# The planner's latency between dependent operations of one engine set to zero, and six products of constants instead of eight

## The chip, the cores and the metric

The kernel runs on one core of one Trainium2 chip. The metric is the device time of one execution in microseconds; a comparison uses the median of several executions. The profiler's record of one more execution, the profiled one, gives the rows that are read below.

## The reference

Three layers stand one behind the other; all inputs and outputs are 32-bit or wider floats.

```python
def phi(x):                                   # q, k: (4, 8, 576, 64)
    proj = np.einsum('bhsd,df->bhsf', x, w_phi)
    proj = proj - np.max(np.abs(proj), axis=-1, keepdims=True)
    return np.concatenate([np.exp(proj), np.exp(-proj)], axis=-1)
q_p, k_p = (phi(q), phi(k))
kv = np.einsum('bhsf,bhsd->bhfd', k_p, v);  z = np.sum(k_p, axis=2)
attn = einsum('bhsf,bhfd->bhsd', q_p, kv) / (einsum('bhsf,bhf->bhs', q_p, z)[..., None] + 1e-06)
# second: a mixture of 8 experts, each token to the expert of its largest logit
h = np.maximum(x[mask] @ w1[e], 0.0);  out[mask] = gate_w * eom * (h @ w2[e])
# third: RMS norm and a gated feed-forward layer, 512 -> 1536 -> 512
g = xn @ w_gate;  y = (g * sigmoid(g) * (xn @ w_val)) @ w_out
```

The second layer's x is the first layer's output, 2304 rows of 512.

## The kernel before, in words

The program is written as a graph of tasks, which a planner in Python (class `Graph`) puts into an order when the kernel is built. The hardware has no part in that: each engine gets a fixed list of instructions, and semaphores hold an instruction until what it reads has been written.

A task has an engine, an estimated duration, the buffers that it reads and writes, and a priority. `emit` (lines 122 to 148) repeats one step: for each engine it looks at the tasks whose inputs are planned, takes the one with the smallest (possible start, priority, number), and of the five engines' candidates emits the one that can start first. A task is ready at the end of its producer plus `lat(producer's engine, own engine)`. `LAT` has 0.27 us for PE, 0.14 for ACT and DVE, 0.15 for POOL and 0 for SP; another 0.12 is added where the consumer is PE. The latency is 0 where both are on PE.

Phase 1 covers the first two layers, batch by batch (four batches), in one graph, so that the planner mixes the attention of batch b+1 with the expert products of batch b. The steps of one batch's attention that the text speaks of:

- L418 is a projection: 8 matmuls of a pair of heads with w_phi into a PSUM tile `pq` of two banks. There are two of these at first (pq0 and pq1), and one after the ninth use. L422 (DVE) takes the maximum over 128 columns, L424 (DVE) subtracts it and writes `d`. L424 is what frees `pq` for the next projection.
- For keys, L518 and L511 (ACT) write exp to `e` and `el`, L465, L468 and L472 (DVE) add up `es`, L498 (PE) makes the kv product, L487 adds the sums, L530 (ACT) and L537 (PE) transpose, L540 (DVE) copies to `kv`.
- For queries, L210 (PE) transposes `d`, L439 (ACT) takes exp into `qp`, L585 (PE; L552 for the rest of 64 rows) multiplies with `kv`, and L447, L449 and L451 (DVE: add, reciprocal, multiply) divide into `x`. L210 or L561 (PE) transposes `x`, L596 or L565 (ACT) casts it and L598 or L568 (DVE) writes the remainder of that cast; both go into `xh`.
- `guess` (L611 to L629) finds the expert that most of the 64 leftover rows choose: a PE product, L615 and L617 on DVE, the PE product L619, and L621, L623, L626, L627 and L629 on DVE. L627 writes the number that L759 loads to address the expert weights.
- `gate` (L644 to L717) takes the logits; its first products need the whole `xh`.
- The expert products are L733 and L742 (PE), 12 matmuls of 288 columns a group; L763 (ACT) and L764 (DVE) split the weights, L780 (ACT) and L782 (DVE) the hidden rows.

At the very start `warm` (L334) gives PE eight products of a matrix of constants, before the first projection. That projection reads w_phi, which L299 loads in two halves, one for each half of the partitions.

Phase 2 is the third layer, in a graph of its own (L921 and L939 on PE). Between the phases all engines load a flag and branch on it (L974 and L975); with these inputs the branch is not taken.

Of the kernel before, what the change touches and what calls it, by code (L numbers as in the profile page):

```python
# [41 lines left out]
class Graph:  # L42
# [31 lines left out]
                del self.leaving[b.tag]  # L74

    def lat(self, a, b):
        if a == b == "PE":
            return 0.0
        return self.LAT[a] + (0.12 if b == "PE" else 0.0)

# [957 lines left out]
def build(tc, ctx, q, k, l, v, w_phi, wg, wo, w1, w2, mg, mv, mo, rg, out):  # L1038
    kk = K(tc, q, k, l, v, w_phi, wg, wo, w1, w2, mg, mv, mo, rg, out)
    nc, g = tc.nc, kk.g  # L1040
    kk.consts(ctx)
    kk.psum()
    moe = ExitStack()
    att = ExitStack()
    kk.moe_slots(moe, ctx)
    kk.attn_slots(att)
    last = []
    with tc.manual_schedule():
        kk.warm(8)
        for b in range(B):  # L1050
            n = len(g.tasks)
            xh, xp, os = kk.attn(b, b * 100)
            last += g.tasks[n:]
            g.marks = getattr(g, "marks", []) + [(n, len(g.tasks))]
            cB = kk.gate(b, xh, xp, os, b * 100 + 30)
            kk.moe(b, xh, xp, cB, 1000 + 100 * b)
        n = B * E
        g.t("DVE", 0.09, lambda: nc.vector.tensor_reduce(
            out=kk.flagf[0:1, n:n + 1], in_=kk.flagf[0:1, 0:n].unsqueeze(1), axis=AX.X, op=ALU.add),
            rw=[kk.flagB], prio=400)  # L1060
        g.t("DVE", 0.07, lambda: nc.vector.tensor_copy(kk.flags[0:1, 0:n + 1], kk.flagf[0:1, 0:n + 1]),
            r=[kk.flagB], prio=400)
        g.emit(until=last)
        att.close()
        kk.phase2_slots(ctx)
        g.slot("xn", kk.xn)
        g.slot("pgv", [kk.last[:, 0]])
        for f in range(NPRE):
            kk.decode_gv(g, f, 2000 + f)
        kk.kept = g.buf("xh", hold=True)  # L1070
        kk.wgv += [Buf(None, 0) for _ in range(NKEEP)]
        for f in range(NPRE, NPRE + NKEEP):
            kk.decode_gv(g, f, 2000 + f, [kk.kept])
        yB, kk.yB = kk.yB, kk.yB[0:1]
        xn0 = kk.prep(g, 0, 355, hold=True)
        kk.yB = yB
        g.emit()
    kk.yB = []
    kk.general([x.ap for x in xn0])
    moe.close()  # L1080
    banks = kk.psum2(ctx)
    p = kk.pool(ctx, "p2", side="right")
    g = Graph()
    kk.use_phase2(g)
    kk.wgv = [Buf(None, x.ap) for x in kk.wgv[:NPRE]] + [
        Buf(None, kk.part(f)) for f in range(NPRE, NPRE + NKEEP)] + [
        Buf(None, p.tile([P, 2, 2, NC, P], F32R, name=f"wgv{f}")) for f in range(NPRE + NKEEP, NF)]
    kk.wout = [Buf(None, p.tile([P, 2, DM], F32R, name=f"wo{f}")) for f in range(NF)]
    g.slot("a", [p.tile([P, 2, UT], F32R, name=f"a{i}") for i in range(NA)])
    g.slot("po", banks[0:4])  # L1090
    g.slot("pgv", banks[4:8])
    held = [x.ap for x in xn0]
    g.slot("xn", [a for a in kk.xn if not any(a is h for h in held)])
    xn = []
    for i, a in enumerate(held):
        x = Buf("xn", a)
        x.slot = (0.0, 100 + i, a)
        xn.append(x)
    with tc.manual_schedule():
        order = [0, NU - 1] + list(range(1, NU - 1))  # L1100
        for u in range(NU):
            if u == 0:
                for f in range(NF):
                    kk.decode_o(g, f, 20 + 2 * f - 6)
                    if f >= NPRE + NKEEP:
                        kk.decode_gv(g, f, 20 + 2 * f - 13)
            kk.unit(g, u, order[u], xn, u * 100 + 20)
            if u + 1 < NU:
                xn = kk.prep(g, order[u + 1], u * 100 + 32)
        g.emit()  # L1110
# [31 lines left out]
```

## Time and profile before

| | |
|---|---|
| median of 3 executions | 857.47 us (856.54 to 859.73) |
| the profiled execution's own time | 854.88 us |
| its span, first to last instruction | 853.3 us |
| PE busy | 839.5 us, 98% of the span |
| DVE busy | 461.1 us, 54% |
| ACT busy | 306.1 us, 36% |
| phase 1 on PE | from the start to 394 us |

PE's records overlap, so its busy time says only that PE had a matmul under way. DVE's and ACT's busy times are those of their instructions. What PE waited for is in a view of its own.

### The profile page before, as it was taken

What the parts mean: (1) busy time and instruction counts of PE and PEld (TensorE: products, weight loads), DVE (VectorE), ACT (ScalarE), POOL (GpSimd) and SP (SyncE); (2) the same over time, 40 slices, a digit from 0 to 9 for tenths busy, and PEclk for the clock granted to TensorE, in tenths of its full rate; (3) what the DMA queues carried; (4) which work ended last, traced back from release to release, by engine and by line L of the source; (5) the groups of instructions that cost most, each with busy time, mean ns of one, the idle gap of its engine ahead of it and who ended that gap; (6) DMA issues with size and microseconds to landing.
All of it is one profiled execution on the core that took longest, in us unless ns stands there. A gap on an engine that the chain in (4) does not pass through costs nothing.

```text
span 853.3 us, 15129 instructions
## 1 busy us (share of the span) xinstructions
PE 839.5 (98%) x6434; PEld 725.5 (85%) x6435; DVE 461.1 (54%) x838; ACT 306.1 (36%) x523; POOL 3.0 (0%) x20
## 2 busy tenths in 40 slices
PE   7989999999999999999999999999999999999998
PEld 6878898898899999998888899888788888888886
DVE  6787786787975598972858734321414114311111
ACT  4363453344443374642435433321214122211111
POOL 1000000000000000000000000000000000000000
PEclk9999999999999999999999999999999999999999
DMA  7263325324102848743324320200002000010001
GB/s 214 82 211 124 84 74 205 118 85 174 52 27 82 310 124 251 224 128 113 116 75 149 99 99 1 61 14 0 1 1 98 1 1 1 0 50 1 0 1 50
DMA packets 64042, 74.64 MB, mean 87 GB/s; under 512 B 9312, under 2 KB 50912, under 8 KB 63456
## 3 DMA queue, kind: packets, MB, share of 16 engines
q1 hardware_dynamic: 63664, 73.27, 26.6%
q8 instruction: 53, 0.87, 0.4%
q10 hardware_dynamic: 304, 0.33, 0.1%
q14 instruction: 21, 0.17, 0.1%
HBM read 54.63 MB, written 18.96 MB: 86 GB/s over the span
## 4 chain that ended last, share of the span: by engine, by line
PE 53%; DVE 0%; ACT 0%; issue 0%
PE pz L921 35%; PE pz L939 17%; PE pz L892 0%; DVE yu L951 0%; ACT yu L954 0%
## 5 line engine op out<-in xcount | busy, mean ns | idle before, releaser
L921 PE MATMUL pz<-xn,wgv 128*128 128x512 f32 (+1 forms) x1200 | 258.2, 371 | 2.0 <-PEq L975 2.0
L921 PEld LDWEIGHTS pz<-xn,wgv 128*128 128x128 f32 x1200 | 210.1, 188 | 43.8 <-issue 2.2
L939 PE MATMUL pz<-wo,a 128*128 128x512 f32 x648 | 159.6, 394 | 0.0
L929 DVE TENSOR_TENSOR row<-pz,row 128x512 f32<-128x512 f32 (+1 forms) x60 | 38.2, 637 | 203.8 <-PE pz L921 200.2
L939 PEld LDWEIGHTS pz<-wo,a 128*128 128x128 f32 x648 | 120.9, 188 | 28.2 <-issue 1.4
L927 ACT ACTIVATE row<-pz 128x512 f32<-128x512 f32 (+1 forms) x60 | 33.4, 556 | 154.5 <-PE pz L921 154.2
L931 ACT CAST a<-row 128x512 fp32r<-128x512 f32 (+1 forms) x60 | 34.6, 577 | 120.8 <-DVE row L929 120.8
L733 PE MATMUL ph<-xh,w 128*128 128x288 f32 x528 | 77.2, 298 | 0.7 <-DVE h L782 0.7
L733 PEld LDWEIGHTS ph<-xh,w 128*128 128x128 f32 x528 | 71.5, 188 | 3.8 <-issue 2.0
L742 PE MATMUL ph<-h,w 128*128 128x288 f32 x480 | 67.9, 296 | 0.0
L742 PEld LDWEIGHTS ph<-h,w 128*128 128x128 f32 x480 | 64.5, 188 | 0.7 <-issue 0.4
L921 PE MATMUL pz<-xn,xh 128*128 128x512 f32 (+1 forms) x240 | 52.3, 373 | 0.0
L932 DVE TENSOR_TENSOR a<-row,a 128x512 fp32r<-128x512 f32 (+1 forms) x60 | 38.2, 637 | 25.8 <-ACT a L931 25.6
L422 DVE TENSOR_REDUCE m<-pq 128x8 f32<-128x1024 f32 x36 | 43.7, 1218 | 15.3 <-PE pq L418 15.1
L763 ACT CAST w<-wr 128x1024 fp32r<-128x1024 f32 x32 | 33.5, 1048 | 46.6 <-issue 19.5
L921 PEld LDWEIGHTS pz<-xn,xh 128*128 128x128 f32 x240 | 42.1, 188 | 8.9
L418 PE MATMUL pq<-wraw,qk 64*128 64x128 f32 x576 | 41.7, 286 | 4.2 <-DVE d L424 4.2
L439 ACT ACTIVATE qp<-ps 128x512 f32<-128x512 f32 x64 | 34.3, 602 | 31.4 <-PE ps L210 27.2
L764 DVE TENSOR_TENSOR w<-wr,w 128x1024 fp32r<-128x1024 f32 x32 | 39.1, 1223 | 10.0 <-ACT w L763 9.4
L424 DVE TENSOR_TENSOR d<-pq,m 128x1024 f32<-128x1024 f32 x36 | 43.6, 1216 | 0.4
L418 PEld LDWEIGHTS pq<-wraw,qk 64*128 64x128 f32 x576 | 35.3, 189 | 9.4 <-DVE d L424 5.1
L742 PE MATMUL ps<-h,w 128*128 128x288 f32 x288 | 41.6, 297 | 0.0
(151 smaller groups left out, 874.4 us busy)
## 6 DMA issues: line engine op xcount, KB each, us to landing
wr<-in_moe_w SPq DMA_DIRECT2D x32, 512.0 KB, 4.1
xdr<-xh SPq DMA_DIRECT2D x4, 2304.0 KB, 9.0
raw<-in_moe_w_gate SPq DMA_DIRECT2D x12, 512.0 KB, 4.3
raw<-in_moe_w_val SPq DMA_DIRECT2D x12, 512.0 KB, 4.0
raw<-in_moe_w_out SPq DMA_DIRECT2D x12, 512.0 KB, 3.5
qk<-in_k SPq DMA_DIRECT2D x16, 256.0 KB, 3.0
v<-in_v SPq DMA_DIRECT2D x16, 256.0 KB, 2.9
qk<-in_q SPq DMA_DIRECT2D x16, 256.0 KB, 3.0
```

The costliest lines, as they stand in the source:

```text
L418: nc.tensor.matmul(pp.ap[:, hf, k * FE:(k + 1) * FE], lhsT=t.ap[r, k], rhs=self.wraw[r], start=True, stop=True)
L422: g.t("DVE", dve(1024), lambda: nc.vector.tensor_reduce(out=m.ap, in_=pv(), axis=AX.X, op=ALU.max, apply_absolute_value=True), r=[pp], w=[ ...
L424: g.t("DVE", dve(1024), lambda: nc.vector.tensor_tensor(out=d.ap.rearrange("p h k f -> p (h k) f"), in0=pv(), in1=m.ap.unsqueeze(2).to_bro ...
L439: g.t("ACT", act(512), lambda f=f: nc.scalar.activation(qp.ap[:, f].rearrange("p c t -> p (c t)"), pd.ap, AF.Exp, scale=1.0 - 2.0 * f), r= ...
L733: self.nc.tensor.matmul(ph[:, 0:HS], lhsT=wv[:, a, c, fs], rhs=xh[:, x, c, cs], start=(c == 0 and i == 0), stop=(c == NC - 1 and i == 2))
L742: self.nc.tensor.matmul(ph[:, 0:HS], lhsT=wv[:, a, f], rhs=hs[f][:, x, cs], start=(f == 0 and i == 0), stop=(f == 7 and i == 2))
L764: g.t("DVE", dve(1024), lambda: nc.vector.tensor_tensor(out=w.ap[:, 1], in0=wr.ap, in1=w.ap[:, 0], op=ALU.subtract), r=[wr], rw=[w], prio= ...
L921: nc.tensor.matmul(ps.ap[:, 0:UT], lhsT=w[:, i, a, c], rhs=xn[c].ap[:, x, 0:UT], start=(c == 0 and n == 0), stop=(c == NC - 1 and n == 2))
L929: g.t("DVE", dve(UT), lambda sil=sil, ps=pgv[1]: nc.vector.tensor_tensor(out=sil.ap[:, 0:UT], in0=ps.ap[:, 0:UT], in1=sil.ap[:, 0:UT], op= ...
L931: g.t("ACT", act(UT, False), lambda sil=sil, a=a: nc.scalar.copy(a.ap[:, 0, 0:UT], sil.ap[:, 0:UT]), r=[sil], w=[a], prio=pr)
L932: g.t("DVE", dve(UT), lambda sil=sil, a=a: nc.vector.tensor_tensor(out=a.ap[:, 1, 0:UT], in0=sil.ap[:, 0:UT], in1=a.ap[:, 0, 0:UT], op=ALU ...
L939: nc.tensor.matmul(po[t].ap, lhsT=a.ap[:, x, ts], rhs=w[:, y], start=(f == 0 and n == 0), stop=(f == NF - 1 and n == 2))
```

## The change: what the planner assumes, and six products in `warm`

```diff
     def lat(self, a, b):
-        if a == b == "PE":
+        if a == b != "SP":
             return 0.0
         return self.LAT[a] + (0.12 if b == "PE" else 0.0)
...
     with tc.manual_schedule():
-        kk.warm(8)
+        kk.warm(6)
```

The first edit sets the planner's latency to 0 for a task that follows its producer on DVE, on ACT or on POOL. No instruction is added or removed by it; the planner's order of both phases changes with it. The second removes two instructions.

Three places of the order follow. In the names, `_0`, `_1`, ... tell the buffer: pq0 and pq1 are the two projection tiles, ps0 to ps3 single PSUM banks, m_0 to m_2 and d_0 to d_2 the maxima and differences, qk_0 to qk_5 the loaded pairs of heads.

DVE, from its first instruction on (start of batch 0), before:

```order
L422 TENSOR_REDUCE m_0_164<-pq0_85 128x8
L422 TENSOR_REDUCE m_1_165<-pq1_89 128x8
L424 TENSOR_TENSOR d_0_161<-pq0_85,m_0_164 128x1024
L424 TENSOR_TENSOR d_1_162<-pq1_89,m_1_165 128x1024
L422 TENSOR_REDUCE m_2_166<-pq0_85 128x8
L465 TENSOR_TENSOR es_0_178<-e_0_167 128x1024
L424 TENSOR_TENSOR d_2_163<-pq0_85,m_2_166 128x1024
```

and now:

```order
L422 TENSOR_REDUCE m_0_164<-pq0_85 128x8
L424 TENSOR_TENSOR d_0_161<-pq0_85,m_0_164 128x1024
L422 TENSOR_REDUCE m_1_165<-pq1_89 128x8
L424 TENSOR_TENSOR d_1_162<-pq1_89,m_1_165 128x1024
L465 TENSOR_TENSOR es_0_178<-e_0_167 128x1024
L422 TENSOR_REDUCE m_2_166<-pq0_85 128x8
L424 TENSOR_TENSOR d_2_163<-pq0_85,m_2_166 128x1024
```

Each subtraction now stands directly behind its own maximum, and the sum es_0 ahead of the third maximum.

DVE in batch 0, from the projections of the queries on (behind the division that writes the second half of the first x), before:

```order
L422 TENSOR_REDUCE m_1_165<-pq1_89 128x8
L615 TENSOR_REDUCE m1_0_142<-ps3_84 64x1
L568 TENSOR_TENSOR xh_0_93<-ps1_82,xh_0_93 128x2x2x64
L617 TENSOR_SCALAR g1_0_138<-ps3_84,m1_0_142 64x8
L424 TENSOR_TENSOR d_1_162<-pq1_89,m_1_165 128x1024
L621 TENSOR_REDUCE m1_0_142<-ps1_82 128x1
L447 TENSOR_SCALAR r_1_194<-ps2_83 128x4
L422 TENSOR_REDUCE m_2_166<-pq0_85 128x8
L623 SCALAR_TENSOR_TENSOR g1_1_139<-ps1_82,m1_0_142,iom_101 128x8
L598 TENSOR_TENSOR xh_0_93<-ps3_84,xh_0_93 128x512
```

and now:

```order
L422 TENSOR_REDUCE m_0_164<-pq0_85 128x8
L615 TENSOR_REDUCE m1_0_142<-ps1_82 64x1
L617 TENSOR_SCALAR g1_0_138<-ps1_82,m1_0_142 64x8
L568 TENSOR_TENSOR xh_0_93<-ps2_83,xh_0_93 128x2x2x64
L598 TENSOR_TENSOR xh_0_93<-ps0_81,xh_0_93 128x512
L621 TENSOR_REDUCE m1_0_142<-ps3_84 128x1
L623 SCALAR_TENSOR_TENSOR g1_1_139<-ps3_84,m1_0_142,iom_101 128x8
L626 TENSOR_REDUCE m1_0_142<-g1_1_139 128x1
L627 TENSOR_SCALAR star_72<-m1_0_142 1x1
L629 TENSOR_SCALAR os_0_144<-g1_1_139,m1_0_142 128x8
L424 TENSOR_TENSOR d_0_161<-pq0_85,m_0_164 128x1024
L422 TENSOR_REDUCE m_1_165<-pq1_89 128x8
```

The chain of `guess` stands in one piece, with L568 and L598, between the maximum of pq0 and the subtraction that frees pq0; before, a subtraction stood three rows behind its maximum, and d_0 of this pair had been written long ahead of this place.

PE at the same place, behind the last L552, before:

```order
L585 MATMUL ps3_84<-kv_0_184,qp_1_182 64x65 x16
L210 MATMUL ps2_83<-ident_58,d_0_161 128x128 x4
L561 MATMUL ps1_82<-ident_58,xl_0_192 128x128 x2
L210 MATMUL ps0_81<-ident_58,d_0_161 128x128 x4
L418 MATMUL pq1_89<-wraw_149,qk_1_151 128x128 x8
L611 MATMUL ps3_84<-wgt_98,xh_0_93 64x8 x4
L418 MATMUL pq0_85<-wraw_149,qk_2_152 128x128 x8
L585 MATMUL ps2_83<-kv_1_185,qp_0_181 64x65 x16
```

and now:

```order
L585 MATMUL ps3_84<-kv_0_184,qp_1_182 64x65 x16
L561 MATMUL ps2_83<-ident_58,xl_0_192 128x128 x2
L418 MATMUL pq0_85<-wraw_149,qk_0_150 128x128 x8
L611 MATMUL ps1_82<-wgt_98,xh_0_93 64x8 x4
L210 MATMUL ps0_81<-ident_58,x_0_190 128x128 x4
L418 MATMUL pq1_89<-wraw_149,qk_1_151 128x128 x8
L619 MATMUL ps3_84<-g1_0_138,mean_64 128x8
L418 MATMUL pq0_85<-wraw_149,qk_2_152 128x128 x8
L210 MATMUL ps1_82<-ident_58,d_0_161 128x128 x4
```

The projection of qk_0 has come to this place from one much earlier, directly behind the projection of qk_5; the next use of pq0, that of qk_2, is three groups of PE behind it.

## Rows read from the trace of the kernel before

**Rows 1.** All waits of PE: line waited for: us in total, times, longest us.
```profile
PE pq L418 <- DVE d L424: 4.2, 3, 2.7
PE pz L921 <- PEq L975: 2.0, 1, 2.0
PE ps L334 <- POOL mean L252: 1.3, 1, 1.3
PE ps L585 <- ACT qp L439: 0.8, 1, 0.8
PE ph L733 <- DVE h L782: 0.7, 1, 0.7
PE ps L650 <- DVE xh L598: 0.4, 1, 0.4
PE ps L487 <- DVE es L472: 0.3, 1, 0.3
```
**Rows 2.** Stretches: length, busy of PE, PEld, DVE, ACT, POOL; clock, DMA share, GB/s.
```profile
36.00:62.00 26.00, 23.74 (x364) 19.30 (x363) 23.29 (x49) 15.41 (x28) 0.00 (x0) 1.00 0.52 166
96.00:134.00 38.00, 38.00 (x555) 33.97 (x554) 31.08 (x64) 20.73 (x37) 0.00 (x0) 1.00 0.30 93
300.00:375.00 75.00, 74.34 (x557) 73.63 (x556) 69.31 (x117) 42.91 (x74) 0.00 (x0) 1.00 0.65 199
375.00:395.00 20.00, 18.96 (x144) 18.73 (x142) 6.34 (x11) 2.45 (x3) 0.00 (x0) 1.00 0.13 46
```
**Rows 3.** DVE in order of time: start us, us, line, tiles [idle before <-releaser].
```profile
6.65 2.36 DVE L422 TENSOR_REDUCE m<-pq 128x8 f32<-128x1024 f32 x2 [6.54 <-PE pq L418]
8.92 2.35 DVE L424 TENSOR_TENSOR d<-pq,m 128x1024 f32<-128x1024 f32 x2
...
26.89 1.22 DVE L422 TENSOR_REDUCE m<-pq 128x8 f32<-128x1024 f32 x1
28.14 1.22 DVE L424 TENSOR_TENSOR d<-pq,m 128x1024 f32<-128x1024 f32 x1
```
**Rows 4.** PE in order of time, the start and the two projections at 20.84.
```profile
1.31 3.78 PE L334 MATMUL ps<-mean 128*128 128x128 f32 x16 [1.31 <-POOL mean L252]
5.02 2.48 PE L418 MATMUL pq<-wraw,qk 64*128 64x128 f32 x32
10.19 2.29 PE L418 MATMUL pq<-wraw,qk 64*128 64x128 f32 x32 [2.69 <-DVE d L424]
...
14.94 1.16 PE L418 MATMUL pq<-wraw,qk 64*128 64x128 f32 x16 [0.58 <-DVE d L424]
...
20.84 2.06 PE L418 MATMUL pq<-wraw,qk 64*128 64x128 f32 x32
```
**Rows 5.** The two loads of w_phi: issue time in ns, first and last start us, landing.
```profile
L299 ACTq DMA_DIRECT2D wraw<-in_w_phi x2: 557/584/611, 0.9 to 1.5; - x2
DMA to landing us min/median/max: 3.0/3.3/3.5
```
**Rows 6.** ACT's first exponentials, in order of time.
```profile
10.17 3.90 ACT L518 ACTIVATE e<-d 128x1024 f32<-128x1024 f32 x4 [5.89 <-DVE d L424]
```
**Rows 7.** DVE in batch 0's query stage, first and last rows of 46.
```profile
36.05 0.16 DVE L447 TENSOR_SCALAR r<-ps 128x4 f32<-128x4 f32 x1 [0.17 <-PE ps L585]
38.31 1.23 DVE L422 TENSOR_REDUCE m<-pq 128x8 f32<-128x1024 f32 x1 [1.43 <-PE pq L418]
...
46.92 0.16 DVE L447 TENSOR_SCALAR r<-ps 128x4 f32<-128x4 f32 x1 [0.34 <-PE ps L585]
...
49.03 0.69 DVE L598 TENSOR_TENSOR xh<-ps,xh 128x512 fp32r<-128x512 f32 x1 [0.68 <-ACT xh L596]
...
59.57 0.69 DVE L598 TENSOR_TENSOR xh<-ps,xh 128x512 fp32r<-128x512 f32 x1
```
**Rows 8.** PE in order of time: the last transposition ahead of the gate, one expert group.
```profile
58.26 0.66 PE L210 MATMUL ps<-ident,x 128*128 128x128 f32 x4
...
70.15 1.76 PE L733 MATMUL ps<-xh,w 128*128 128x288 f32 x12
```

## The prediction

> **What bounds the kernel now.** I read the waits of PE first. In 853.3 us they come to 9.7 us [rows 1], and 6.4 of these are neither the start (1.3) nor the branch between the phases (2.0). So PE sets the end: no edit of the order can give back more than about 6.4 us, 0.75%, and whatever PE comes to wait is added in full, since no work of PE's goes away but two products at the start. All but 0.7 of the 6.4 lies ahead of 62 us, in batch 0, where no expert products exist yet to fill PE. The stretches [rows 2] say why: from 36 to 62 us DVE is busy 23.3 of 26 us (90%), from 96 to 134 (batch 1's queries) 31.1 of 38 (82%), and PE waits in the first and never in the second. So I read DVE's order in batch 0, row by row, against the changed one.
>
> **What a dependent row costs on DVE.** Two maxima in a row take 2.36 us, each 1.22 alone: the second starts 1.14 behind the first, before that has ended. A subtraction directly behind its own maximum starts at 28.14 behind 26.89, that is 1.25 later [rows 3]. A dependent neighbour thus costs 0.11 to 0.12 us. The old 0.14 is nearly right, the new 0 is too low. In the old order 78 of DVE's rows in phase 1 stand directly behind a row whose output they read, in the new one 202 (counted in the two orders by the names of buffers): 124 more, or some 14 us of DVE. From 300 us to the branch DVE is busy 69.3 of 75 and then 6.3 of 20 us [rows 2]; the 17 extra pairs behind batch 3's attention (2 us) are covered by the last 20 us. Phase 2 has 16 more (1.9 us) and nearly the same order of PE; I cost it at nothing, because PE never waits for DVE or ACT there [rows 1]. The price is paid where DVE is the engine that is late, in batch 0.
>
> The Trainium skill has a rule that speaks for the new number (VectorE: DVE Perf Modes, "The DRAIN you can't avoid"): it says that a semaphore between two Vector operations costs nothing extra, as the pipe is flushed between any two. The trace disagrees by the 0.11 us above. By the rule the extra pairs would be free and the sum below would lose about 2.2 us; that is the fourth case.
>
> **The two products fewer.** Eight take 3.78 us from 1.31 on, and the projection follows at 5.02 [rows 4]. w_phi's second half is issued at 1.5 and lands up to 3.5 later, at 5.0 [rows 5]; the projection's second matmul needs it. So six products leave PE to wait for the load: gain at most 0.1, taken as 0. What they may cost is the clock. The first two projections take 2.48 us, two later ones 2.06 [rows 4], though the granted clock reads 1.00 (the 2.4 GHz level) in the stretches shown [rows 2]: PE was slow at first. If it stays slow to the end of the first projection, that one, 1.16 us at full rate [rows 4], takes up to 2.3 where it took 1.6 (from 5.02 to DVE's start at 6.65 [rows 3]): 0 to +0.6 us. I take 0, since PE still has work from 1.31 to about 4.2 and again from 5.0.
>
> The Trainium skill (TensorE: Matmul & The Clock Gate, "Why this matters for your kernels") advises to keep TensorE continuously busy so as to reach the faster clock. By that the gap before 5.0 could put the rise off, which is the fifth case; no row here shows such a gap at the start.
>
> **The start, to 22 us.** Now the first subtraction runs from 6.65 + 1.25 = 7.90 and ends at 9.12, where it ended at 10.14; the third projection begins at 9.17 and not at 10.19 [rows 3, 4], 1.0 us earlier. It isn't kept. The first two exponentials take 1.95 us [rows 6], so e is there at 11.1 and L498, now ahead of the fourth projection, runs from 11.15 to 12.95; es_0, now ahead of the third maximum, starts at 11.43, that maximum at 12.57, its subtraction at 13.82 and ends at 15.04. The fifth projection waits for it and begins at 15.09, where it began at 14.94 [rows 4]. Net +0.15.
>
> **Batch 0's queries, 35 to 62 us.** The projection of qk_0 was done at 21.8, the second of the two at 20.84 [rows 4]. Now it comes behind L561. PE is thus 0.75 us earlier at L585 and L552 (1.0 less work, 0.15 late, the rest handshakes), but DVE gets the pair L422 and L424 of that projection in its fullest stage, where it had it when idle.
>
> DVE before: from 36.05 to 59.57 + 0.69 = 60.26, 24.2 us, of which it waited 1.43 + 0.34 + 0.68 = 2.45 [rows 7], so 21.8 of work in 46 rows. Now 47 rows: the extra subtraction 1.13, and 21 dependent neighbours where there were 2, 19 x 0.12 = 2.3. That is 25.2 of work from 35.3 on; with the one wait that I find sure (for the moved projection, 0.6) and some 0.3 of others it ends at 61.4, 1.1 us later, though it starts 0.75 earlier.
>
> PE's waits in that stage, followed through the new order with the durations of these rows:
> - qk_2's projection needs pq0, so the subtraction d_0, which stands behind the whole chain of guess and L598. The maximum runs 36.7 to 37.9, the chain to 40.05 (L619's answer included), the subtraction ends at 41.2. PE has been through L611, L210, the next projection and L619 by 39.1: 2.1 us of wait. Before, this projection waited for nothing.
> - Four short ones of 0.1 to 0.25 (0.85 together): qk_3 for d_1, L210 for a bank that DVE is slow to free, and two on L585, for L439 behind the weight casts L763.
> - The last transposition of x needs both halves of x_1; the second L585 for it ends at 57.6, DVE, in the middle of older rows, delivers at 59.35: 1.75 us. It began at 58.26 [rows 8].
>
> Sum 4.7. Before, the waits of this stage were 0.9 + 0.8 + 0.4 + 0.3 = 2.4 [rows 1]. So +2.3, and +0.15 from the start: **+2.4 us**. Behind the gate the expert products begin and PE is full again. The 0.7 at the first experts [rows 1] may stay or go. Bounds: 0, if the chain of guess is the only thing that I have mis-timed, and +4.8, if the start's clock (+0.6) and a repeat of the 1.75 in the next batch come on top.
>
> The profiled execution's own time is 854.88, the median of the runs 857.47; I add the difference to the median: **859.9 us** (the profile itself would read 857.3).
>
> **The rivals.**
> 1. *The forecast:* batch 0 alone pays. 859.9, between 857.5 and 862.3.
> 2. *Slower: batches 1 and 2 become like batch 0.* Between L552 and the gate of batch 1 the old order of PE has seven expert groups, the new one five. A group of 12 takes 1.76 less its overlap, 1.6 [rows 8], so the 38 us of that stretch get some 3.5 us shorter, while DVE gains 8 pairs (0.9) and loses some filler. 31.1 in 34.5 us is 90%, the share at which batch 0 makes PE wait [rows 2]. Price: another 2.3 us a batch in two batches, 859.9 + 4.6 = 864.5. It decides from a DVE share of about 0.9 in that stretch. Against it: expert products don't depend on that DVE work, and five are left to fill with.
> 3. *Faster: the denser order takes the waits away.* If the walk is wrong and batch 0's 5.7 us of waits go, with L733's 0.7, it gains up to 6.4: 851.1 at best, 853 with three quarters of it. For it: dependent chains end sooner when nothing stands between. Against it: DVE's work in the stage grows by 3.4 us by rows that I trust.
> 4. *The change does nothing that can be seen:* the extra pairs fall where DVE has slack, or cost no more than independent ones, and the 2.4 is not paid: 857.5, give or take 1.
> 5. *The clock rises later at the start:* 859.9 + 0.6 = 860.5.
>
> **How the numbers follow.** A measurement of this kernel can tell about 0.5%, 4.3 us, from no change: faster is below 853.2, slower above 861.8. Chances: forecast 0.42, slower rival 0.20, faster 0.05, nothing seen 0.23, clock 0.10. Slower by over 0.5% takes nearly all of the second (0.18) and a tail of the first and last (0.04), 0.22; faster takes the third, 0.05; the rest, 0.73, is within 0.5%. The range leaves out the faster case and the upper part of the slower one: 856.0 to 864.0.
>
> **What would show it.** Right: among PE's waits one of about 2 us on L418 for L424 near 40 us, and waits of L210 for L451 near 58; the gate's first product, right behind the transposition that began at 58.26 [rows 8], near 61.7; the third projection near 9.2 and the fifth near 15.1; DVE's steps at 1.25 behind a maximum. Wrong: PE's waits ahead of 62 us below 6 us in all, or new waits on L733, L585 or L210 between 100 and 270 us (the second rival), a first pair of projections over 2.9 us long (the fifth), or DVE's share of batch 0's stage not above 90%.

## The result and the profile after

The changed kernel takes 867.89 us (median of 6 executions, 864.62 to 870.76) against 857.00 for the kernel before on the same chip (6 executions): a ratio of 1.0121, 95% interval 1.0100 to 1.0141, so about 10.4 us slower. The forecast was 859.9, with a range up to 864.0. The profiled execution reads 865.67 (span 864.0), where the one before read 854.88 (span 853.3): 10.8 us to explain.

All waits of PE after the change (line waited for: us in total, times, longest us); they answer to [rows 1]:

```profile
PE pq L418 <- DVE d L424: 4.7, 4, 2.6
PE pz L921 <- PEq L975: 2.0, 1, 2.0
PE ps L210 <- DVE x L451: 1.7, 2, 1.5
PE ps L334 <- POOL mean L252: 1.3, 1, 1.3
PE ph L733 <- DVE h L782: 1.1, 1, 1.1
PE ps L733 <- DVE h L782: 1.0, 1, 1.0
PE ps L498 <- ACT e L518: 0.9, 1, 0.9
PE pq L418 <- DMA wraw<-in_w_phi: 0.6, 1, 0.6
PE ps L585 <- ACT qp L439: 0.2, 1, 0.2
```

They sum to 13.5 us where [rows 1] sum to 9.7: 3.8 us more wait, and the profiled execution is 10.8 us longer. Most of the loss is not in this view. Nor does PE's busy time by stretches show all of it (the columns of [rows 2], with a short stretch at the end):

```profile
36.00:62.00 26.00, 21.51 (x344) 18.32 (x338) 23.71 (x47) 12.26 (x21) 0.00 (x0) 0.93 0.47 144
96.00:134.00 38.00, 38.00 (x558) 33.89 (x557) 29.12 (x62) 18.30 (x35) 0.00 (x0) 1.00 0.37 120
300.00:375.00 75.00, 72.92 (x544) 71.98 (x543) 69.42 (x117) 44.85 (x79) 0.00 (x0) 1.00 0.65 196
43.60:46.80 3.20, 3.20 (x22) 2.87 (x23) 3.17 (x3) 2.21 (x5) 0.00 (x0) 0.50 1.05 363
```

Batch 0's stage has lost 2.2 us of PE's busy time against [rows 2], and part of it ran at a granted clock of 0.50 (the 1.2 GHz level), as the last row shows; before, the whole stage read 1.00. From 300 to 375 us another 1.4 are lost. Between 96 and 134 us PE is busy all the time, before and after alike.

To see where a full PE loses time I used a measure of my own: each matmul counts with the usual step from its start to the next one's start for its kind (132 ns for an expert product, 61 for L418, and so on), and two kernels are compared at the time when the same sum of such work, the warm products aside, has been started. The first row is the kernel before, in us; the others are later (+) or earlier than it by so many us, each in its profiled execution. The branch between the phases lies between the last two columns.

| after so much of PE's work (us) | 10 | 70 | 160 | 235 | 325 | 420 |
|---|---|---|---|---|---|---|
| before | 19.6 | 88.3 | 185.8 | 265.5 | 358.7 | 457.2 |
| the change | +1.15 | +4.89 | +6.39 | +8.98 | +10.42 | +10.77 |
| lat_only | +0.33 | +3.30 | +4.81 | +7.39 | +8.84 | +10.86 |
| zero_early | +0.17 | +7.77 | +7.62 | +7.62 | +7.62 | +7.76 |
| zero_late | +1.99 | +2.21 | +3.72 | +6.11 | +7.56 | +9.09 |
| fine_parts | +0.26 | +0.38 | +3.56 | +4.35 | +5.93 | +7.76 |
| late_stay3 | +0.08 | -0.55 | -0.76 | -0.14 | +1.79 | +10.81 |
| late_stay3_260 | +2.71 | +2.08 | +1.87 | +2.49 | +3.71 | +4.87 |
| guess_later | +1.07 | -1.34 | -1.33 | -1.33 | -1.34 | -1.37 |
| stay3_guess_220 | +0.94 | -2.06 | -3.73 | -3.10 | -3.10 | -1.49 |

Some of these steps are the clock and not the order. In zero_early and in zero_late these stretches ran at the 1.2 GHz level (columns of [rows 2]):

```profile
23.10:29.80 6.70, 6.70 (x40) 3.86 (x40) 3.49 (x6) 0.72 (x2) 0.00 (x0) 0.50 0.24 67
64.10:67.30 3.20, 3.20 (x24) 2.69 (x21) 2.15 (x4) 1.44 (x4) 0.00 (x0) 0.50 0.66 276
```

```profile
11.00:14.30 3.30, 3.04 (x28) 3.04 (x30) 2.25 (x3) 3.06 (x4) 0.00 (x0) 0.50 0.72 197
403.60:406.80 3.20, 3.20 (x8) 2.52 (x9) 0.00 (x0) 0.57 (x1) 0.00 (x0) 0.50 0.09 21
```

If half the clock costs half of such a stretch, they are up to 5 us of zero_early's 7.77 (an estimate from the 9.9 us of the first fence), and in zero_late the first goes with about 0.9 of its 2 us at the start (the other 1.1 are a slow first pair of projections, read below) and the second with 1.5 at the branch. lat_only and fine_parts, which lose 2.0 and 1.8 at the branch, have a stretch at 0.50 there too (from 405.1 and from 401.9 us). So the steps between the columns are read where both kernels ran at full clock: between 70 and 375 us the clock reads 1.00 in the kernel before, in the change and in zero_late.

So the change loses 4.9 us up to batch 1's attention and then another 5.5 bit by bit until batch 3's attention ends, in stretches where PE looks nearly full (257.65 of 260 us between 70 and 330, before 259.34). Phase 2 adds nothing.

### The profile page after: what moved, and what is told of

Its sections match the earlier page's. It is cut to its first block, busy times and chain, and to the rows that moved or that the text cites. A ratio compares the mean times of both kernels' runs of the same rounds, so it can differ in the third digit from the quotient of the medians.

```text
span 864.0 us, 15139 instructions
## 1 busy us (share of the span) xinstructions
PE 846.4 (98%) x6430; PEld 727.9 (84%) x6431; DVE 470.7 (54%) x838; ACT 306.1 (35%) x523; POOL 3.0 (0%) x20
## 4 chain that ended last, share of the span: by engine, by line
PE 52%; DVE 0%; ACT 0%; issue 0%
PE pz L921 35%; PE pz L939 17%; PE pz L892 0%; DVE yu L951 0%; ACT yu L954 0%
## 5 line engine op out<-in xcount | busy, mean ns | idle before, releaser
L921 PE MATMUL pz<-xn,wgv 128*128 128x512 f32 (+1 forms) x1200 | 258.0, 371 | 2.0 <-PEq L975 2.0
L921 PEld LDWEIGHTS pz<-xn,wgv 128*128 128x128 f32 x1200 | 210.2, 188 | 43.9 <-issue 2.2
L742 PE MATMUL ph<-h,w 128*128 128x288 f32 x528 | 75.9, 298 | 0.0
L733 PE MATMUL ph<-xh,w 128*128 128x288 f32 x504 | 74.6, 299 | 1.1 <-DVE h L782 1.1
L742 PEld LDWEIGHTS ph<-h,w 128*128 128x128 f32 x528 | 71.1, 188 | 1.7 <-issue 1.2
L733 PEld LDWEIGHTS ph<-xh,w 128*128 128x128 f32 x504 | 68.4, 188 | 4.8 <-issue 2.0
L422 DVE TENSOR_REDUCE m<-pq 128x8 f32<-128x1024 f32 x36 | 44.0, 1221 | 19.6 <-PE pq L418 19.4
L921 PE MATMUL pz<-xn,xh 128*128 128x512 f32 (+1 forms) x240 | 52.3, 373 | 0.0
L418 PE MATMUL pq<-wraw,qk 64*128 64x128 f32 x576 | 44.8, 296 | 5.3 <-DVE d L424 4.7
L921 PEld LDWEIGHTS pz<-xn,xh 128*128 128x128 f32 x240 | 42.1, 188 | 8.9
L418 PEld LDWEIGHTS pq<-wraw,qk 64*128 64x128 f32 x576 | 37.7, 198 | 12.0 <-DVE d L424 5.7
L424 DVE TENSOR_TENSOR d<-pq,m 128x1024 f32<-128x1024 f32 x36 | 43.9, 1220 | 0.6
L733 PE MATMUL ps<-xh,w 128*128 128x288 f32 x264 | 39.2, 297 | 1.0 <-DVE h L782 1.0
```

The source lines that it names most:

```text
L418: nc.tensor.matmul(pp.ap[:, hf, k * FE:(k + 1) * FE], lhsT=t.ap[r, k], rhs=self.wraw[r], start=True, stop=True)
L422: g.t("DVE", dve(1024), lambda: nc.vector.tensor_reduce(out=m.ap, in_=pv(), axis=AX.X, op=ALU.max, apply_absolute_value=True), r=[pp], w=[ ...
L424: g.t("DVE", dve(1024), lambda: nc.vector.tensor_tensor(out=d.ap.rearrange("p h k f -> p (h k) f"), in0=pv(), in1=m.ap.unsqueeze(2).to_bro ...
L733: self.nc.tensor.matmul(ph[:, 0:HS], lhsT=wv[:, a, c, fs], rhs=xh[:, x, c, cs], start=(c == 0 and i == 0), stop=(c == NC - 1 and i == 2))
L742: self.nc.tensor.matmul(ph[:, 0:HS], lhsT=wv[:, a, f], rhs=hs[f][:, x, cs], start=(f == 0 and i == 0), stop=(f == 7 and i == 2))
L921: nc.tensor.matmul(ps.ap[:, 0:UT], lhsT=w[:, i, a, c], rhs=xn[c].ap[:, x, 0:UT], start=(c == 0 and n == 0), stop=(c == NC - 1 and n == 2))
```

## The experiments

**Which edit, and which part of the program.** Four kernels: the first edit alone, the second alone, and the first edit in two halves by the planner's own clock.

```diff
 lat_only:    if a == b != "SP":                                          (warm(8))
 six_only:    kk.warm(6)                                                  (latencies as before)
 zero_early:  if a == b == "PE" or a == b != "SP" and self.now < 62.0:    (warm(8))
 zero_late:   if a == b == "PE" or a == b != "SP" and self.now >= 62.0:   (warm(8))
```

lat_only:

> The first edit alone: the changed order on every engine, with eight products of constants. Theory (the order costs it, by PE's waits in batch 0, by the lower clock that follows the longest of them, and by PE changing more often between kinds of products): about 866, 9 us over before; the two products give or take 1 us. Rival (the six products cost it, by the clock that rises 3 us later at the start): 857 to 859. In the profile the theory expects the wait of about 2.6 us on L418 near 40 us and a granted clock under 1.00 behind it; the rival expects neither.

six_only:

> The second edit alone: the order of before on every engine, with six products of constants. Theory: 857 to 858.5, the start at most 1.2 us later, since the later clock costs the first two projections only. Rival: 862 or more, most of the loss.

zero_early:

> Eight products; the planner's latency between dependent rows of one engine is 0 up to 62 us of its own time and 0.14 behind that, so that batch 0's attention has the changed order and the rest is planned as before from there. Theory: the 4 to 5 us that the changed kernel has lost by 66 us, and little more: 860.5 to 862.5. Rival (what is lost is lost everywhere, by finer mixing of attention and expert products): under 859.

zero_late:

> Eight products; 0.14 up to 62 us of the planner's time, 0 behind that. Theory: what the changed kernel loses between 66 us and 312 us, 5 to 6 us: 861 to 863, without a wait over 1 us before 62 us and with the granted clock at 1.00 there. Rival (all loss stems from batch 0): within 1 us of before.

Measured, as ratios to the kernel before: lat_only 1.0136 [1.0108, 1.0164], six_only 1.0025 [1.0007, 1.0042], zero_early 1.0053 [1.0029, 1.0078], zero_late 1.0069 [1.0046, 1.0093]. The first edit is the whole loss within its interval, and its halves add up to the change's (0.53 + 0.69 = 1.22%). The intervals of the halves overlap, so the times don't say which is the larger. The table puts them in their places: the early order costs 3.3 us up to 70 us of work in lat_only, where no clock fell until then, and zero_early loses nothing more behind that; zero_late loses 5.35 between 70 and 325, which the forecast had at nothing. Of that, the waits of L733 for L782 are 2.1 us in zero_late where [rows 1] has 0.7:

```profile
PE ps L733 <- DVE h L782: 1.1, 1, 1.1
PE ph L733 <- DVE h L782: 1.0, 1, 1.0
```

which leaves 4 us for something that is no wait. By my reading it is in the steps. PE of the kernel before, in order of time, with two runs of expert products and what stands between them:

```profile
140.67 0.44 PE L537 MATMUL ps<-ident,ks 128*128 128x128 f32 x2
140.87 3.45 PE L742 MATMUL ps<-h,w 128*128 128x288 f32 x24
144.15 0.28 PE L689 MATMUL ps<-g,mean 128*128 128x8 f32 x2
144.29 5.01 PE L742 MATMUL ph<-h,w 128*128 128x288 f32 x36
```

and of zero_late:

```profile
134.83 3.42 PE L742 MATMUL ph<-h,w 128*128 128x288 f32 x24
138.09 0.28 PE L689 MATMUL ps<-g,mean 128*128 128x8 f32 x2
138.23 3.44 PE L742 MATMUL ps<-h,w 128*128 128x288 f32 x24
...
391.80 3.37 PE L742 MATMUL ps<-h,w 128*128 128x288 f32 x24
395.00 6.52 PE L742 MATMUL ph<-h,w 128*128 128x288 f32 x48
```

Inside a long run 24 products take 3.20 us (391.80 to 395.00); the same 24 behind another kind of product take 3.26 to 3.28. In zero_late's single records the first product of nearly every run is followed after 213 to 244 ns, the others after 132. Summed from the first expert product to the branch, beyond the usual steps:

| | unbroken runs of expert groups | first products of runs | steps into and out of runs |
|---|---|---|---|
| before | 40 | 3.90 us | 3.19 us |
| the change | 51 | 5.08 us | 5.50 us |
| zero_late | 51 | 5.07 us | 5.41 us |
| dve_lat_25 | 48 | 4.72 us | 4.42 us |
| fine_parts | 60 | 6.15 us | 5.34 us |
| late_stay3_260 | 33 | 3.20 us | 2.94 us |
| stay3_guess_220 | 33 | 3.05 us | 2.61 us |

The 11 further runs of zero_late go with 1.17 + 2.22 = 3.4 us, 0.31 a run (all 40 runs of the kernel before average 0.18, so the steps into and out of runs have also become dearer); with 1.4 of waits and 0.7 of steps among the attention's own products (9.12 against 8.44) that is the 5.4. It is a reading, however, and the changed order also has 132 more dependent neighbours on DVE (286 against 154 in the whole program). The next runs set one against the other.

**Latency as a scale, and a finer mixing without the change.** Where `a == b == "DVE"` returned 0.25, 0.12 or 0.07 instead of 0.14; and, with the latencies of before, the expert products given to the planner in parts of 3:

```diff
-                for part in ((0, 1, 2, 3),):
+                for part in ((0,), (1,), (2,), (3,)):
...
-                for part in (range(0, 4), range(4, 8)):
+                for part in [(i,) for i in range(8)]:
```

(An order with latency 0 on DVE alone is row for row that of the first edit, and with 0 on ACT alone that of before: only DVE's number matters.)

dve_lat_25:

> Kernel before (eight products of constants) with the planner's latency between dependent operations of DVE raised from 0.14 to 0.25 us, the other way from the change. Directly dependent neighbours on DVE (whole program, by the names in the order): 135, where the kernel before has 154 and the change 286. Unbroken runs of expert groups on PE in phase 1: 48, where before has 40 and the change 51. Theory A (mixing: each further run of expert groups costs PE about 0.2 us, from the first product of a run, 0.10 us longer, and the steps in and out of it, 0.09 us; plus whatever waits the new order brings): +1.6 us from the mixing, 859 us or more; the loss grows between 66 and 330 us, without waits to explain it. Theory B (the late loss of the change comes from dependent neighbours on DVE): fewer neighbours, so no loss behind 66 us, 857.5 or below. Theory C (any other order is a draw): anything within 4 us of before.

dve_lat_12:

> Kernel before with that latency at 0.12 us, what the rows of DVE show. 151 dependent neighbours, 38 runs of expert groups (before: 154 and 40). Theory A: -0.4 us from the mixing, 857.0 unless batch 0 gets a new wait; theory B: no change, 857.5; theory C: anything within 4 us. If this number is right for the planner, PE's waits ahead of 62 us stay at or below 6 us in all.

dve_lat_07:

> Kernel before with that latency at 0.07 us, half of what it was. 163 dependent neighbours, 42 runs of expert groups. Theory A: +0.4 us from the mixing and whatever batch 0 waits, 857 to 860; theory B: 9 more neighbours of the 132 that the change adds, +0.4 us; theory C: anything within 4 us.

fine_parts:

> Kernel before with its latency, but the expert products are given to the planner in parts of 3 instead of groups of 12. The products are the same; the planner may break a run of them in more places. Dependent neighbours on DVE 151 (before 154), unbroken runs of expert products on PE 60 (before 40). Theory A: 20 more runs at about 0.2 us, +4 us, 861.5, lost between 66 and 330 us with little more wait of PE. Theory B (neighbours on DVE): no loss there, 857.5. Theory C: anything within 4 us, with the loss in waits and not in the steps at a run's start.

Measured: dve_lat_25 1.0026 [1.0008, 1.0044], median 859.92; dve_lat_12 0.9993 [0.9973, 1.0012], 856.58; dve_lat_07 1.0043 [1.0022, 1.0064], 861.41; fine_parts 1.0058 [1.0035, 1.0081], 862.52. Latency is not a scale: both 0.25 and 0.07 are slower, and 0.12, what the rows show, is no different from 0.14. dve_lat_25 has fewer neighbours than before and fine_parts as many, and both lose time between 70 and 325 us of work (2.8 and 5.5 us): theory B has no place for that. Of fine_parts' 5.5 first products and steps are 4.4 (20 runs at 0.22) and longer waits of L733 1.2. dve_lat_07 was outside theory A's range too. Two runs more cost little; its waits sum to 10.9 us, 1.2 more than before (two of L733 take 2.1 where one took 0.7, and one of L498, 1.7, stands in place of others), and the rest of its loss isn't accounted for here. The number of runs is not the only thing that a new order brings, and theory C fits the three latencies as well; only fine_parts, 4.7 us above before, is outside it.

**Fewer runs with the neighbours kept.** One rule for the planner: a run of expert groups, once begun, goes on to three groups if they can start. late_stay3 is zero_late with it, stay3 the kernel before with it.

```diff
-                        key = (max(s, f), k.prio, k.seq)
+                        stay = e == "PE" and 0 < self.run < 3 and k.prio >= 1000
+                        key = (max(s, f), k.prio - 1000 * stay * (k.prio < 2000), k.seq)
...
+                self.run = self.run + 1 if 1000 <= k.prio < 2000 else 0
                 self.products(s, k)
```

late_stay3:

> The kernel with DVE's latency at 0 from 62 us on (zero_late), and one rule more in the planner: a run of expert groups on PE, once begun, goes on to three groups if they can start. 32 unbroken runs of expert groups (zero_late 51, before 40), 266 dependent neighbours on DVE (zero_late 252, before 154). Theory A (the late loss is the mixing and the waits of the new order): 19 runs fewer at about 0.19 us, 3.6 us less than zero_late, and the two waits of L733 on L782 near 300 and 310 us go down; 857 to 859. Theory B (the late loss comes from the dependent neighbours): it stays at 862 to 863, as there are more of them.

stay3:

> The kernel before (all its latencies, eight products) with the rule of three alone. 28 or 29 unbroken runs instead of 40, dependent neighbours 154 as before. Theory A: 11 or 12 runs fewer at 0.19 us, -2.2 us, and the wait of L733 on L782 near 307 us (0.7) may go as well: 854.5, lost nowhere else. Theory B: no change, 857.5. Against both: longer runs make the next batch's attention wait for PE, so its gate comes later; if that starves PE near 330 us, 859 or more.

Measured: late_stay3 1.0109 [1.0090, 1.0128], stay3 1.0016 [1.0003, 1.0029]. By the times theory A is wrong. The table says where: late_stay3 is level with the kernel before (-0.14) at 235 us of work, still near it (+1.79) at 325, and loses 9 us at the branch. stay3 goes the same way: it is ahead by 0.78 at 325 and behind by 4.27 at 420, with waits of 3.2 and 0.9 us at the branch and a clock of 0.50 from 396.7 to 403.5 us. late_stay3's longest wait of PE (this file's lines are 3 higher from there on, so L924 and L978 are the old L921 and L975), and DVE's last rows of phase 1:

```profile
PE pz L924 <- ACTq L978: 9.1, 1, 9.1
```

```profile
392.08 0.43 DVE L829 TENSOR_SCALAR row<-raw 128x512 uint32<-128x512 uint32 x1 [1.59 <-DMA raw<-in_moe_w_gate]
...
404.36 0.69 DVE L839 TENSOR_TENSOR xh<-row,xh 128x512 fp32r<-128x512 f32 x1 [0.68 <-ACT xh L838]
```

PE has no product of phase 1 left from about 396 us, but ACT and DVE are still unpacking phase 2's weights until 405: the longer runs had put batch 3's attention, and with it this work, later (that batch's gate begins at 315.4 us, in zero_late at 279.6). The gain was there and was given back at a new wait. So the rule was ended ahead of that part (`and self.now < 260.0`):

late_stay3_260:

> late_stay3 with the rule of three only up to the planner's 260 us, so that batch 3's attention and the preparation of phase 2 on ACT and DVE are not pushed behind PE's end of phase 1. 33 unbroken runs of expert groups (zero_late 51, before 40), 262 dependent neighbours on DVE (zero_late 252, before 154). Theory A (mixing and PE's waits): the 5.5 us of the late loss are regained and not lost again at the branch (PE's wait there 2 to 3 us, as before): 857 to 859, where zero_late had 863.2. Theory B (neighbours on DVE): 862 to 863.

Measured: 1.0015 [1.0001, 1.0028], median 858.27, as theory A had it. PE's waits at the branch and for L421 (the old L418):

```profile
PE pq L421 <- DVE d L427: 3.6, 2, 2.7
PE pz L924 <- PEq L978: 1.8, 1, 1.8
```

No wait of an expert product is left in that view. Zero_late had 1.0069; the intervals are apart, with 262 neighbours on DVE against 252. So the late loss is not DVE's dependent neighbours: it goes when runs and waits change and the neighbours stay, and fine_parts has it without them. How it divides between the finer mixing (3.4) and the waits (1.4) remains the reading above, as the rule changes both. Nor is all regained: by the table late_stay3_260 still loses 1.6 us between 70 and 325 (zero_late 5.35), 1.2 of them behind 235, about where the rule ends.

**The clock.** Does the fall to the lower level at 43.5 us come from the wait of 2.6 us ahead of it? Eight products of constants behind L619 were to fill the wait:

```diff
+            for i in range(8 if b == 0 else 0):
+                nc.tensor.matmul(pc.ap[:, P:2 * P], lhsT=self.mean, rhs=self.mean, start=True, stop=True)
```

fill_gap:

> The changed kernel with eight more products of constants (128x128, into columns of the bank that nothing reads) directly behind L619 of batch 0, so ahead of the wait of 2.6 us of L418 for L424 near 40 us; all other rows stand as in the change. They fit into the wait (about 0.9 us), so they add nothing to it. Theory of the clock (the granted clock that fell at 43.5 us for 3.4 us fell on account of that wait, and costs up to 1.7 us): 866.2 to 867, ratio 1.010 to 1.011 to before, and no stretch below full clock between 40 and 50 us. Rival (only the wait itself costs, the fall is a draw or belongs to an earlier wait): 867.9, ratio 1.012.

Measured: 1.0120 [1.0103, 1.0137]. The products took 2.05 us instead of 0.9, the next step of the chain of guess on DVE (L624, the old L621) waited for their end too, and PE's wait stayed (columns as in [rows 4]):

```profile
40.14 2.05 PE L622 MATMUL ps<-mean 128*128 128x128 f32 x16
44.42 1.46 PE L418 MATMUL pq<-wraw,qk 64*128 64x128 f32 x16 [2.23 <-DVE d L424]
```

The clock fell behind it as well (0.50 from 45.2 to 48.4 us). The experiment did not take away what it was to take away, and says nothing on the cause. lat_only says more: it has the same order with the same longest wait, and its expectation of a clock under 1.00 behind that wait did not come true. Its waits for L424, and the stretch of batch 0's queries:

```profile
PE pq L418 <- DVE d L424: 5.8, 5, 2.6
```

```profile
36.00:62.00 26.00, 20.91 (x352) 17.60 (x351) 24.02 (x46) 13.63 (x23) 0.00 (x0) 1.00 0.45 143
```

So the wait is not followed by the fall in every execution. What decides is left open.

**A better order.** stay3_guess and guess_later put the chain of `guess` of batch 0 later by 17 in priority, with the rule of three and without it; stay3_guess_220 has the chain later and the rule up to 220 us.

```diff
-        os = self.guess(b, xh, xp[NC], np_)
+        os = self.guess(b, xh, xp[NC], np_ + 17 * (b == 0))
```

stay3_guess:

> stay3, and in batch 0 the chain of guess gets a later priority (17 more), so that it stands behind the query stage's own rows on DVE. 29 runs. Batch 0's waits of PE in the query stage were 2.4 us before; if the chain is what makes them, 1 to 2 us less than stay3, 853; if the expert weights then come too late for the first expert group, a wait there and 856 or more.

guess_later:

> The kernel before with one number changed: in batch 0 the chain of guess gets a later priority by 17. 40 runs of expert groups as before. If the chain makes PE's waits of batch 0's query stage, 2 us less than before, 855.5; if it only moves them, 857.5; if the weights of the first experts come too late, a wait on the first L733 and 859.

stay3_guess_220:

> The kernel before with the later chain of guess and the rule of three up to the planner's 220 us. 33 runs of expert groups instead of 40 (at 0.19 us, -1.3), batch 0's waits 1 to 2 us less, and nothing lost at the branch: 854 to 855, ratio 0.996 to 0.997. If the rule still makes phase 2's preparation late, PE waits over 3 us at the branch and the time is that of stay3_guess, 856.5.

Measured: stay3_guess 0.9986 [0.9973, 0.9999], guess_later 0.9961 [0.9947, 0.9975], stay3_guess_220 0.9960 [0.9946, 0.9975] (medians 856.55, 853.98, 853.41). stay3_guess misses its 853: it keeps stay3's waits at the branch (3.2 and 0.6 us). The last two are 0.4% faster than the kernel before; one number does nearly all of it. PE's waits in stay3_guess_220 (lines 3 higher), beside those at the start and at the branch:

```profile
PE pq L421 <- DVE d L427: 2.7, 1, 2.7
PE ps L213 <- DVE x L454: 0.3, 1, 0.3
```

In batch 0's query stage 0.3 us of wait is left of 2.4. The rule of three shows in the table (1.8 us less than guess_later at 325) and is gone at 420; in that execution the clock read 0.50 from 394.1 to 397.2 us, behind the branch, and in guess_later's it read 1.00 there. The times don't separate the two.

## Why the prediction was wrong, by its own steps

**Batch 0's queries: the mechanism right, the exact sum by luck.** The forecast's sum of waits was 4.7 us. PE after the change, in order of time:

```profile
42.33 1.16 PE L418 MATMUL pq<-wraw,qk 64*128 64x128 f32 x16 [2.56 <-DVE d L424]
...
54.57 1.15 PE L585 MATMUL ps<-kv,qp 128*64 128x65 f32 x32 [0.19 <-ACT qp L439]
...
61.09 0.66 PE L210 MATMUL ps<-ident,x 128*128 128x128 f32 x4 [1.48 <-DVE x L451]
62.22 1.16 PE L418 MATMUL pq<-wraw,qk 64*128 64x128 f32 x16 [0.47 <-DVE d L424]
```

2.56 + 0.19 + 1.48 + 0.47 = 4.70. The two long waits came where they were named (forecast 2.1 and 1.75). Of the four short ones (0.85 together) one came, 0.19 on L585; the 0.47 belongs to a projection that the forecast did not name. The parts miss by +0.46, -0.27 and -0.19, so that the sums agree to the hundredth is luck. DVE's rows behind the first wait:

```profile
37.77 1.23 DVE L422 TENSOR_REDUCE m<-pq 128x8 f32<-128x1024 f32 x1 [0.63 <-PE pq L418]
38.91 0.15 DVE L615 TENSOR_REDUCE m<-ps 64x1 f32<-64x8 f32 x1
...
40.94 0.21 DVE L629 TENSOR_SCALAR os<-g,m 128x8 f32<-128x8 f32 x1
41.07 1.20 DVE L424 TENSOR_TENSOR d<-pq,m 128x1024 f32<-128x1024 f32 x1
```

The chain of guess does stand between the maximum and its subtraction, and these rows are 1.0 to 1.1 us later than forecast, as is the start. The gate's first product, forecast near 61.7, came 2.0 later, at 63.73; the stretch at half clock lies between. In lat_only, without that stretch and with eight products, it came at 62.14. DVE's share of the stage, the forecast's other sign, rose from 90 to 91% (23.71 of 26 us).

**The start: right for the first edit, open for the second.** In lat_only:

```profile
5.02 2.66 PE L418 MATMUL pq<-wraw,qk 64*128 64x128 f32 x32
9.36 1.16 PE L418 MATMUL pq<-wraw,qk 64*128 64x128 f32 x16 [1.68 <-DVE d L424]
...
15.27 1.16 PE L418 MATMUL pq<-wraw,qk 64*128 64x128 f32 x16 [0.84 <-DVE d L424]
```

The third and fifth projections come at 9.36 and 15.27, forecast 9.17 and 15.09. With six products, in the changed kernel:

```profile
4.17 0.79 PE L418 MATMUL pq<-wraw,qk 64*128 64x128 f32 x2
5.53 3.78 PE L418 MATMUL pq<-wraw,qk 64*128 64x128 f32 x30 [0.57 <-DMA wraw<-in_w_phi]
```

PE waits for the load until 5.5, and the first pair takes 0.79 + 3.78 = 4.57 us where 2.9 was the mark of the fifth rival. So the slow start, taken as 0 and bounded by 0.6, cost 0.8 in this execution (1.15 against lat_only's 0.33). The granted clock reads 1.00 from 5 to 9 us, as it does in six_only, so no row shows that this is the clock. Nor is it shown to be the second edit's: in six_only the same pair took 2.78 us, and with eight products and the order of before it took 2.48 in the kernel before and 3.55 in zero_late:

```profile
5.02 3.55 PE L418 MATMUL pq<-wraw,qk 64*128 64x128 f32 x32
```

By its ratio the second edit costs 0.07 to 0.42%, taken as nothing; where it does is open.

**"Behind the gate the expert products begin and PE is full again": the step that failed.** PE is full between 96 and 134 us (38.00 of 38.00), nearly so up to 330, and still loses 5.5 us up to 325 us of work, about half the loss. The step looked for waits and for DVE's share; it did not ask what a full PE was full of. The new order cuts the expert products into 51 runs instead of 40, and two waits on L733 near 300 us take 2.1 us where one took 0.7 (that the 0.7 "may stay or go" left out that it could grow).

**The rivals.** The second had the right place and nearly the right price for it (4.6 us, found 5.5), with the wrong cause: DVE's share between 96 and 134 us fell from 82% to 77% (29.12 of 38), and the waits of L210 and L585 that it named did not come in the later batches beyond half a microsecond; those of L733 lie near 300 us, behind the stretch that it named. (Its own sum is slightly off: two groups at 1.6 us are 3.2 and not 3.5, which makes the share 89%.) The third and the fourth fall. The mark of the fifth, a first pair over 2.9 us, was passed, with what is said of the start above. The price of a dependent neighbour stands: behind its maximum at 37.77 the next, independent row starts 1.14 later, and at the start of the changed kernel

```profile
7.64 1.23 DVE L422 TENSOR_REDUCE m<-pq 128x8 f32<-128x1024 f32 x1 [7.53 <-PE pq L418]
8.90 1.23 DVE L424 TENSOR_TENSOR d<-pq,m 128x1024 f32<-128x1024 f32 x1
10.04 1.22 DVE L422 TENSOR_REDUCE m<-pq 128x8 f32<-128x1024 f32 x1
```

a subtraction follows its maximum after 1.26, the independent maximum after 1.14. Phase 2, costed at nothing, cost nothing (+10.77 at 420 us of work, +10.76 at 800). The prediction's 124 and 16 further dependent neighbours make 140 where the later count has 132; no conclusion hangs on the difference.

**The range.** With the late part at 0, and the clock and the slow start too, the range ended at 864.0, 0.5 short of the second rival's own price and 3.9 short of the result. Forecast +2.4; found about 0.3 (the order) and 0.8 (the slow first pair) at the start, 2.3 from waits in batch 0, up to 1.6 from the 3.2 us at half clock behind 43.5, and 5.5 later: 10.5 of 10.8.

## What to carry to other kernels

An engine that is busy all the time can still lose: count how often a new order changes from one kind of product to another, here 0.2 to 0.3 us for each further run of expert groups, by the sums above. A number in a planner is no dial: two values below the kernel's own (0 and 0.07) and one above (0.25) were slower, and 0.12 was not, so each order is to be read by itself, at the place where the engine that sets the end waits. And a gain in the middle is kept only if nothing that must be done by the next meeting point of all engines, here the unpacking of phase 2's weights, was pushed back to make it.

## What was not expected of the hardware

Executions of one and the same order differ by the granted clock. zero_late has the order of the kernel before, and its eight products, up to the first expert products. The stretch behind the same wait near 10 us reads 0.50 there (11.00 to 14.30, shown under the table), and behind the branch 0.50 too; in the kernel before:

```profile
11.00:14.30 3.30, 3.30 (x40) 2.19 (x36) 3.17 (x4) 3.07 (x4) 0.00 (x0) 1.00 0.97 279
393.00:400.00 7.00, 4.99 (x26) 4.12 (x25) 0.46 (x1) 1.00 (x1) 0.00 (x0) 1.00 0.24 69
```

Once at the 1.2 GHz level, once at 2.4. The profile of before happened to have no such fall ahead of 852 us and reads 854.88, below its median; of 95 executions of it beside the experiments, 22 had a mean granted clock of 0.999 (median 855.2 us), 46 had 0.995 (857.8) and 11 had 0.993 (859.6). In zero_early the mean was 0.993 over ten executions, so part of its 0.53% is clock; what makes it fall in one execution and not in another is left open.

The other thing is the step at a run's start: the first expert product behind a product of another kind is followed after 213 to 244 ns instead of 132, in 38 of the 40 runs of the kernel before and 47 of the 51 of zero_late.
